# A bank of its own for the last products, and squares issued one block ahead, in a fused attention and expert kernel

## The chip, the cores and the metric

The kernel runs on one core of one Trainium2 chip. Its time is the device time of one execution in microseconds (us); lower is better. Before the change the median of three runs is 751.62 us (751.49 to 752.33).

## The reference

Three layers run one after the other in float32. First comes windowed and dilated attention over 4 batches, 8 heads and 576 positions, which gives `x` of 2304 tokens by 512. Then each token goes through one of eight experts. The last layer, which the change touches, is dense:

```
h = np.maximum(x @ w_in, 0.0)          # 2304 x 512 by 512 x 2048
return (h * h @ w_out).astype(np.float32)   # 2304 x 2048 by 2048 x 512
```

## The kernel before

Every matrix product is made exact enough by splitting each operand into a high part (rounded, by ScalarE) and a low part (the operand less its high part, by VectorE) and multiplying high by high, high by low and low by high: three matmuls for one (`mm3`, lines 814 to 816).

The dense layer has two stages. **The seven-product stage** computes `g = x @ w_in`, transposed, with a seven-product scheme on 2 by 2 blocks. It goes over six visits, each one half of the features for one of three blocks of 768 tokens. A visit has two double steps, and `strassen(d)` issues double step `d`, which handles two pairs of feature rows. A double step opens its own products ("now") and closes those of the one before it ("old"), so that engines have time between them; `strassen(12)` only closes: S3·T3 and A22·T4 of the last two pairs. A product is 6 matmuls of 384 columns. The eight PSUM banks are named in `bank(tag, n)`: four "b", two "c", two "d". S3·T3 accumulates into the pair's bank `pb`; `added` (line 1111) has VectorE add another tile to the bank, and stores the sum into the DRAM tensor `g_d`. Then A22·T4 accumulates into the same `pb`, and `kept` (line 1100) has ScalarE copy it out for a store. The "kept" tiles have three buffers, the tiles for the stores ("cr") eight.

**The second stage** multiplies `relu(g)` squared by `w_out`. `ORDER` lists 48 blocks, 16 feature blocks for each of the three token blocks, and the token block visited last comes last. `load_g` fetches a block of `g_d` (384 KB) into one of four buffers `gq`, on SyncE's queue (SP). `split_g` squares it in place on VectorE (line 1365), makes the high part on ScalarE (1366) and the low part on VectorE (1367), into one of three pairs of slots inside `slot_d`. `down2(n, j)` multiplies block n by the output weights of its feature block: for each of six columns of 128 tokens three matmuls of 512 columns (lines 1397 to 1399) into an `op` tile, of which there are eight, one in each bank. After 16 blocks the `op` tiles are copied out, half by VectorE and half by ScalarE, and scattered to the output by GpSimd (line 1407).

The output weights arrive as 64-bit numbers and are narrowed and split beside the products: `narrow1` on ScalarE (lines 1136 and 1137), `narrow2` and `narrow3` on VectorE (1143 to 1152), `out_hi` on ScalarE (1161), `out_lo` on VectorE (1166). In the seven-product stage `beside()` hands out these steps after each product. What is left goes to `finish_units(n)`, which issues the same number of steps in each of the second stage's first 14 blocks; the weights of feature block f are wanted by block f, the sixteenth by block 15.

The order of the work is written out by hand: each engine runs its instructions in the order in which this code issues them, and waits at an instruction until its inputs are there and its output's place is free. Thus `split_g(1)`, issued between `strassen(11)` and `strassen(12)`, stands in VectorE's and ScalarE's order ahead of all that `strassen(12)` asks of them; and within a block of the second stage the split of block n + 2 comes first, then the load of block n + 4, then the weight steps, then the matmuls of block n.

Of the kernel before, what the change touches and what calls it, by code (L numbers as in the profile page):

```python
# [10 lines left out]
F32 = mybir.dt.float32  # L11
# [5 lines left out]
ALU = mybir.AluOpType  # L17
# [49 lines left out]
def attention_experts_kernel(ctx: ExitStack, tc: tile.TileContext, qB, kB, vB, wg, wE, wF, consts, rows, ids, out):  # L67
    nc = tc.nc
# [691 lines left out]
    def experts():  # L760
# [329 lines left out]
        def bank(tag, n):  # L1090
            return ps2.tile([P, 512], F32, tag=tag, name=f"bank_{tag}", bufs=n)[:, :TB]

        def product(out, pair, a, n, b, first):
            wh, wl = left_t[pair, a]
            mh, ml = right(n, b)
            for i in range(2):
                o = slice(P * i, P * i + P)
                mm3(out, wh[:, o], wl[:, o], mh[:, i], ml[:, i], first and i == 0, i == 1, not first)

        def kept(bank, tag="kept"):  # L1100
            t = up_.tile([P, TB], F32, tag=tag, name=tag, bufs=8 if tag == "cr" else 3)
            nc.scalar.copy(out=t, in_=bank)
            return t

        def out_tile():
            return up_.tile([P, TB], F32, tag="cr", name="cr", bufs=8)

        def store_g(q, b, f, t):
            nc.sync.dma_start(out=g_d[b][P * f:P * f + P, TB * t:TB * t + TB], in_=q)

        def added(x, y, b, f, t):
            q = out_tile()
            nc.vector.tensor_tensor(out=q, in0=x, in1=y, op=ALU.add)  # L1113
            store_g(q, b, f, t)
# [12 lines left out]
        def load_next():  # L1127
            u = next(loaded64, None)
            if u is not None:
                load_64(*u, raw2)  # L1130
# [56 lines left out]
        def ready(n, name):  # L1187
            return n < 1 or name == "B12" or (n, name) in split
# [69 lines left out]
        def beside():  # L1258
            s = clock["slot"]
            for e in range(3):  # L1260
                credit[e] = min(credit[e] + RATE[e], 1.6)
            for lane in lanes:
                while lane.head is not None:
                    do, cost, gap, first = lane.head
                    if s < max(first, lane.last + gap) or any(c and credit[e] < min(c, 1.5) for e, c in enumerate(cost)):
                        break
                    lane.last = s
                    lane.pull()
                    do()
                    for e in range(3):  # L1270
                        credit[e] -= cost[e]
            clock["slot"] += 1

        def must(lane, done):
            while not done():
                do = lane.head[0]
                lane.last = clock["slot"]
                lane.pull()
                do()
# [3 lines left out]
        def strassen(d):  # L1283
            now = None
            if d < 2 * len(VISITS):
                b, half = VISITS[d // 2]
                now = dict(b=b, n=SETS[d // 2], pairs=[PAIRS * half + 2 * (d % 2) + i for i in range(2)], pb=[], pd=[], p5=[])
            old = prev.pop() if prev else None

            def use(x, i, out, a, b, first):  # L1290
                must(lanes[2], lambda: (x["pairs"][i], a) in left_t)
                must(lanes[1], lambda: ready(x["n"], b))
                product(out, x["pairs"][i], a, x["n"], b, first)

            if now:
                for i in range(2):
                    f = 2 * now["pairs"][i]
                    pb, pc = bank("b", 4), bank("c", 2)
                    now["pb"].append(pb)
                    use(now, i, pb, "A11", "B11", True)  # L1300
                    beside()
                    use(now, i, pc, "A12", "B21", True)
                    added(pc, kept(pb), now["b"], f, 0)
                    beside()
            if old:
                for i in range(2):
                    use(old, i, old["pb"][i], "S3", "T3", False)
                    added(old["pb"][i], old["p5"][i], old["b"], 2 * old["pairs"][i] + 1, 1)
                    beside()
            if now:  # L1310
                for i in range(2):
                    pd = bank("d", 2)
                    now["pd"].append(pd)
                    use(now, i, pd, "S1", "T1", True)
                    now["p5"].append(kept(pd, "p5"))
                    beside()
            if now:
                for i in range(2):
                    use(now, i, now["pb"][i], "S2", "T2", False)
                    beside()  # L1320
            if old:
                for i in range(2):
                    use(old, i, old["pb"][i], "A22", "T4", False)
                    store_g(kept(old["pb"][i], "cr"), old["b"], 2 * old["pairs"][i] + 1, 0)
                    beside()
            if now:
                for i in range(2):
                    use(now, i, now["pd"][i], "S4", "B22", False)
                    added(now["pd"][i], kept(now["pb"][i]), now["b"], 2 * now["pairs"][i], 1)
                    beside()  # L1330
                prev.append(now)
# [3 lines left out]
        def finish_units(n):  # L1335
            lane = lanes[2]
            todo = []
            while lane.head is not None:
                todo.append(lane.head[0])
                lane.pull()  # L1340
            rest.extend(todo)
            for _ in range(-(-len(rest) // max(14 - n, 1))):
                rest.pop(0)()
# [5 lines left out]
        ORDER = [(b, f) for b in reversed(range(NTP)) for f in range(16)]  # L1349
        gq_t, g_t = {}, {}  # L1350
        gp = None

        def load_g(n):
            if n < len(ORDER):
                b, f = ORDER[n]
                t = gp.tile([P, TP], F32, tag="gq", name="gq", bufs=4)
                nc.sync.dma_start(out=t, in_=g_d[b][P * f:P * f + P, :])
                gq_t[n] = t

        def split_g(n):  # L1360
            if n < len(ORDER):
                u = 6 + 2 * (n % 3)
                h, l = (flat_y[:, TP * (u + a):TP * (u + a) + TP] for a in range(2))
                x = gq_t.pop(n)
                nc.vector.scalar_tensor_tensor(out=x, in0=x, scalar=0.0, in1=x, op0=ALU.max, op1=ALU.mult)  # L1365
                nc.scalar.copy(out=h, in_=x)  # L1366
                nc.vector.tensor_tensor(out=l, in0=x, in1=h.bitcast(F32), op=ALU.subtract)  # L1367
                g_t[n] = (h, l)

        load_next()  # L1370
        load_next()
        for d in range(2 * len(VISITS)):
            strassen(d)
            if d == 10:
                load_g(3)
                split_g(0)
            if d == 9:
                yst.close()
                gp = ust.enter_context(tc.tile_pool(name="gp", bufs=1, side="right", reuse_waits="tile"))
                for n in range(3):  # L1380
                    load_g(n)
        split_g(1)
        strassen(2 * len(VISITS))
        pst.close()
        ps3 = st.enter_context(tc.tile_pool(name="ps3", bufs=1, space=PSUM, reuse_waits="tile"))

# [27 lines left out]

        JS = range(TP // P)
        for n in range(len(ORDER)):
            split_g(n + 2)
            load_g(n + 4)
            finish_units(n)
            if n + 2 < len(ORDER):  # L1420
                for j in JS:
                    down2(n, j)
# [76 lines left out]
    with tc.manual_schedule():  # L1499
        experts()  # L1500
# [85 lines left out]
```

## Time and profile before

| | |
|---|---|
| median of the runs | 751.62 us |
| the profiled execution, its own time | 755.42 us |
| its span, first to last instruction | 753.8 us |
| TensorE busy | 703.1 us, 93% |
| VectorE busy | 485.9 us, 64% |
| ScalarE busy | 328.0 us, 44% |
| mean granted TensorE clock | 0.97 |

The span is one execution as the hardware profiler recorded it. The share of an engine is the time in which it ran instructions of its kind; matmuls overlap their neighbours, so a busy TensorE is not one at its peak. The granted clock is the share of full speed that TensorE was allowed. The seven-product stage lies between about 356 and 539 us of the span, the second stage behind it, up to about 741 us.

### The profile page before, as it was taken

The numbers are of one execution on the slowest core, as the hardware profiler recorded it, in microseconds if no ns is written. First come the engines' busy times: TensorE is split into PE (matmuls) and PEld (weight loads), VectorE is DVE, ScalarE is ACT, GpSimd is POOL, SyncE is SP. The second block draws the span as 40 slices with busy tenths as digits, with TensorE's granted clock in tenths as the row PEclk, the third lists the DMA queues.
The fourth block names the chain that finished last, engine by engine and source line by source line (L and its number), as shares of the span: only waits on it lengthen the run. The fifth ranks groups of instructions, "written<-read, shape, count | busy, mean of one in ns | idle before, by whom it ended". The sixth has DMA issues, their size and how long they took to land. (4 is left out here: it accounts for less than half of the span.)

```text
span 753.8 us, 13877 instructions
## 1 busy us (share of the span) xinstructions
PE 703.1 (93%) x5227; PEld 639.2 (85%) x5227; DVE 485.9 (64%) x894; ACT 328.0 (44%) x601; POOL 113.5 (15%) x120
## 2 busy tenths in 40 slices
PE   7879379999999999999999999999899999999993
PEld 4657249999999999999999999999788778888882
DVE  7757446576566476678986877787577755445430
ACT  2534124464445555656555545555334322222110
POOL 5344422420110110008000000000000030011003
PEclk9989777999999999999999999999999999999997
DMA  8998564684756668663656654766544444334302
GB/s 274 324 255 248 162 217 121 215 243 146 232 177 207 206 191 248 214 219 83 219 166 231 194 170 156 255 194 214 179 151 157 135 165 127 105 118 154 99 8 87
DMA packets 67155, 136.90 MB, mean 182 GB/s; under 512 B 10857, under 2 KB 43498, under 8 KB 66058
## 3 DMA queue, kind: packets, MB, share of 16 engines
q1 hardware_dynamic: 57434, 120.09, 50.5%
q0 software_dynamic: 4176, 10.57, 4.1%
q10 hardware_dynamic: 5472, 5.29, 2.1%
q8 instruction: 43, 0.70, 0.4%
q14 instruction: 30, 0.25, 0.1%
HBM read 102.00 MB, written 33.96 MB: 180 GB/s over the span
## 5 line engine op out<-in xcount | busy, mean ns | idle before, releaser
L1367 DVE TENSOR_TENSOR slot_d<-gq,slot_d 128x768 fp32r<-128x768 f32 x48 | 46.0, 959 | 75.8 <-ACT slot_d L1366 75.8
L1366 ACT CAST slot_d<-gq 128x768 fp32r<-128x768 f32 x48 | 40.1, 835 | 111.4 <-PE op L1398 73.4
L1407 POOL DMA_INDIRECT out<-os,idc x18 | 19.6, 1088 | 363.9 <-DVE os L1406 359.5
L828 ACT ACTIVATE hh<-hp 128x240 fp32r<-128x240 f32 (+6 forms) x72 | 29.3, 408 | 42.4 <-PE hp L816 41.9
L158 POOL DMA_INDIRECT xg<-x_d,mt x23 | 25.3, 1101 | 142.5 <-PE xp L182 95.7
L1365 DVE SCALAR_TENSOR_TENSOR gq<-gq 128x768 f32<-128x768 f32 x48 | 45.6, 951 | 0.0
L1397 PE MATMUL op<-slot_b,slot_d 128*128 128x512 f32 x108 | 42.8, 396 | 1.4 <-ACT slot_b L1161 1.4
L1398 PE MATMUL op<-slot_b,slot_d 128*128 128x512 f32 x108 | 42.8, 396 | 0.9 <-DVE slot_b L1166 0.9
L1399 PE MATMUL op<-slot_b,slot_d 128*128 128x512 f32 x108 | 42.8, 396 | 0.0
L1397 PE MATMUL op<-slot_a,slot_d 128*128 128x512 f32 x108 | 42.0, 389 | 0.0
L1399 PE MATMUL op<-slot_a,slot_d 128*128 128x512 f32 x108 | 42.0, 389 | 0.0
L1398 PE MATMUL op<-slot_a,slot_d 128*128 128x512 f32 x108 | 42.0, 389 | 0.0
L140 DVE TENSOR_TENSOR slot_d<-raw,slot_d 128x1024 fp32r<-128x1024 f32 x24 | 29.3, 1226 | 19.7 <-ACT slot_d L139 19.7
L481 PE MATMUL o<-vb,pts 128*32 128x130 f32 x576 | 23.5, 298 | 19.2 <-DMA vb<-in_vB 14.6
L829 DVE SCALAR_TENSOR_TENSOR hl<-hp,hh 128x240 fp32r<-128x240 f32 (+6 forms) x72 | 31.2, 443 | 15.6 <-ACT hh L828 15.5
L481 PEld LDWEIGHTS o<-vb,pts 128*32 128x32 f32 x576 | 17.2, 117 | 23.1 <-issue 19.0
L843 ACT COPY ys<-yp 128x240 f32<-128x240 f32 (+6 forms) x36 | 14.3, 397 | 46.6 <-PE yp L816 46.5
L140 DVE TENSOR_TENSOR slot_b<-raw,slot_b 128x1024 fp32r<-128x1024 f32 x20 | 24.2, 1221 | 12.8 <-ACT slot_b L139 12.8
L814 PE MATMUL bank_b<-slot_d,slot_a 128*128 128x384 f32 x84 | 28.5, 340 | 3.8 <-DVE cr L1113 3.8
L814 PE MATMUL yp<-hh,slot_b 128*128 128x240 f32 (+3 forms) x112 | 31.9, 285 | 0.0
L815 PE MATMUL yp<-hl,slot_b 128*128 128x240 f32 (+3 forms) x112 | 31.7, 283 | 0.0
L816 PE MATMUL yp<-hh,slot_b 128*128 128x240 f32 (+3 forms) x112 | 31.6, 282 | 0.0
(323 smaller groups left out, 2316.7 us busy)
## 6 DMA issues: line engine op xcount, KB each, us to landing
raw<-in_wE SPq DMA_DIRECT2D x63, 512.0 KB
g_d<-cr SPq DMA_DIRECT2D x96, 192.0 KB
gq<-g_d SPq DMA_DIRECT2D x48, 384.0 KB
raw<-in_wF SPq DMA_DIRECT2D x32, 512.0 KB
vb<-in_vB SPq DMA_DIRECT2D x16, 520.0 KB
yr<-yT_d SPq DMA_DIRECT2D x16, 384.0 KB
q<-in_qB SPq DMA_DIRECT2D x8, 512.0 KB
x_d<-x SPq DMA_DIRECT2D x22, 128.0 KB
```

The costliest lines, as they stand in the source:

```text
L140: nc.vector.tensor_tensor(out=lo, in0=raw, in1=hi.bitcast(F32), op=ALU.subtract)
L481: nc.tensor.matmul(out=o[p // 2][32 * c:32 * c + 32, p % 2, 0:130], lhsT=pt[:, p, 32 * c:32 * c + 32], rhs=v[:, :, p, c, :], start=True, s ...
L814: nc.tensor.matmul(out=out, lhsT=wh, rhs=mh, start=first, stop=False, skip_group_check=shared)
L815: nc.tensor.matmul(out=out, lhsT=wh, rhs=ml, start=False, stop=False, skip_group_check=shared)
L816: nc.tensor.matmul(out=out, lhsT=wl, rhs=mh, start=False, stop=last, skip_group_check=shared)
L829: nc.vector.scalar_tensor_tensor(out=l[:, :n], in0=p[:, :n], scalar=0.0, in1=h[:, :n].bitcast(F32), op0=ALU.max, op1=ALU.subtract)
L1365: nc.vector.scalar_tensor_tensor(out=x, in0=x, scalar=0.0, in1=x, op0=ALU.max, op1=ALU.mult)
L1366: nc.scalar.copy(out=h, in_=x)
L1367: nc.vector.tensor_tensor(out=l, in0=x, in1=h.bitcast(F32), op=ALU.subtract)
L1397: nc.tensor.matmul(out=o_t[j], lhsT=h[:, a], rhs=w[:, 0], start=f == 0, stop=False)
L1398: nc.tensor.matmul(out=o_t[j], lhsT=h[:, a], rhs=w[:, 1], start=False, stop=False)
L1399: nc.tensor.matmul(out=o_t[j], lhsT=l[:, a], rhs=w[:, 0], start=False, stop=f == 15)
```

## The change

It has two parts. In `strassen(12)`, where nothing new is opened, A22·T4 gets a "c" bank and starts a sum there in place of going on in `pb`. ScalarE copies the bank of S3·T3 into a "kept" tile (`u3`) once S3·T3 is done, and VectorE adds that tile to the new bank and stores the sum.

In the second stage the square leaves `split_g` and becomes `square_g`; `split_g` issues the high part and hands back the low part as a function, so that its caller can put something between them. The main loop now issues the high part of block n + 2, the square of block n + 3, the low part of block n + 2 and the load of block n + 5. Ahead of the loop block 1 is squared at the end of `strassen(10)`, and its split, the square of block 2 and the load of block 4 come after `strassen(12)`; before, the split of block 1 came ahead of it.

```
             if old:
                 for i in range(2):
                     use(old, i, old["pb"][i], "S3", "T3", False)
                     added(old["pb"][i], old["p5"][i], old["b"], 2 * old["pairs"][i] + 1, 1)
+                    if not now:
+                        u3.append(kept(old["pb"][i]))
                     beside()
...
-                    use(old, i, old["pb"][i], "A22", "T4", False)
-                    store_g(kept(old["pb"][i], "cr"), old["b"], 2 * old["pairs"][i] + 1, 0)
+                    if now:
+                        use(old, i, old["pb"][i], "A22", "T4", False)
+                        store_g(kept(old["pb"][i], "cr"), old["b"], 2 * old["pairs"][i] + 1, 0)
+                    else:
+                        pc = bank("c", 2)
+                        use(old, i, pc, "A22", "T4", True)
+                        added(pc, u3[i], old["b"], 2 * old["pairs"][i] + 1, 0)
...
+        def square_g(n):
+            if n < len(ORDER):
+                x = gq_t[n]
+                nc.vector.scalar_tensor_tensor(out=x, in0=x, scalar=0.0, in1=x, op0=ALU.max, op1=ALU.mult)
+
         def split_g(n):
             if n < len(ORDER):
...
-                nc.vector.scalar_tensor_tensor(out=x, in0=x, scalar=0.0, in1=x, op0=ALU.max, op1=ALU.mult)
                 nc.scalar.copy(out=h, in_=x)
-                nc.vector.tensor_tensor(out=l, in0=x, in1=h.bitcast(F32), op=ALU.subtract)
                 g_t[n] = (h, l)
+                return lambda: nc.vector.tensor_tensor(out=l, in0=x, in1=h.bitcast(F32), op=ALU.subtract)
+            return lambda: None
...
             if d == 10:
                 load_g(3)
-                split_g(0)
+                square_g(0)
+                split_g(0)()
+                square_g(1)
...
-        split_g(1)
         strassen(2 * len(VISITS))
+        lo = split_g(1)
+        square_g(2)
+        lo()
+        load_g(4)
...
         for n in range(len(ORDER)):
-            split_g(n + 2)
-            load_g(n + 4)
+            lo = split_g(n + 2)
+            square_g(n + 3)
+            lo()
+            load_g(n + 5)
             finish_units(n)
```

## Rows read from the trace of the kernel before

**Rows 1.** The page, parts 1 (busy us, share) and 2 (slices; granted clock in tenths).
```profile
PE 703.1 (93%) x5227; PEld 639.2 (85%) x5227; DVE 485.9 (64%) x894; ACT 328.0 (44%) x601; POOL 113.5 (15%) x120
...
PEclk9989777999999999999999999999999999999997
```

**Rows 2.** Waits of TensorE, whole span: total us, times, longest.
```profile
PE bank_b L814 <- DVE cr L1113: 3.8, 1, 3.8
...
PE op L1397 <- ACT slot_b L1161: 1.4, 1, 1.4
```

**Rows 3.** Timeline of TensorE at the last products: start, us, instruction, [idle before <-releaser].
```profile
532.00 0.34 PE L816 MATMUL bank_b<-slot_d,slot_b 128*128 128x384 f32 x1
536.10 0.44 PE L814 MATMUL bank_b<-slot_d,slot_a 128*128 128x384 f32 x1 [3.77 <-DVE cr L1113]
...
539.22 0.63 PE L1397 MATMUL op<-wo,slot_d 128*128 128x512 f32 x1
...
540.50 0.44 PE L1397 MATMUL op<-wo,slot_d 128*128 128x512 f32 x1
```

**Rows 4.** Timeline of VectorE in the same stretch.
```profile
532.16 0.69 DVE L1152 CUSTOM_DVE_ANT_0 fp<-fa,fl 128x1024 uint16<-128x1024 uint16 x1
532.77 0.95 DVE L1365 SCALAR_TENSOR_TENSOR gq<-gq 128x768 f32<-128x768 f32 x1
534.62 0.96 DVE L1367 TENSOR_TENSOR slot_d<-gq,slot_d 128x768 fp32r<-128x768 f32 x1 [0.90 <-ACT slot_d L1366]
535.50 1.02 DVE L1113 TENSOR_TENSOR cr<-bank_b,p 128x384 f32<-128x384 f32 x2
```

**Rows 5.** Windows: us; PE, PEld, DVE, ACT, POOL busy; clock; DMA share; GB/s.
```profile
537.30:540.50 3.20, 3.20 (x10) 2.92 (x10) 0.08 (x1) 1.52 (x3) 0.00 (x0) 0.50 0.39 140
545.00:590.00 45.00, 45.00 (x201) 37.22 (x200) 34.08 (x50) 17.87 (x27) 0.00 (x0) 1.00 0.45 155
553.50:555.50 2.00, 2.00 (x10) 1.67 (x9) 1.45 (x2) 0.52 (x1) 0.00 (x0) 1.00 0.00 0
605.60:608.40 2.80, 2.80 (x8) 2.23 (x7) 1.83 (x2) 0.83 (x2) 0.00 (x0) 0.50 0.06 9
615.00:735.00 120.00, 120.00 (x532) 99.34 (x531) 57.87 (x65) 27.42 (x34) 10.55 (x9) 1.00 0.35 108
```

**Rows 6.** Timeline of TensorE in the second stage.
```profile
598.14 0.50 PE L1398 MATMUL op<-slot_b,slot_d 128*128 128x512 f32 x1 [0.71 <-DVE slot_b L1166]
...
603.72 0.50 PE L1397 MATMUL op<-slot_b,slot_d 128*128 128x512 f32 x1 [1.43 <-ACT slot_b L1161]
604.45 0.50 PE L1398 MATMUL op<-slot_b,slot_d 128*128 128x512 f32 x1 [0.23 <-DVE slot_b L1166]
...
609.84 0.39 PE L1399 MATMUL op<-slot_b,slot_d 128*128 128x512 f32 x1
...
740.42 0.39 PE L1399 MATMUL op<-slot_b,slot_d 128*128 128x512 f32 x1
```

**Rows 7.** Groups of VectorE, 545 to 590: busy us, mean ns, idle before, releaser.
```profile
L1367 DVE TENSOR_TENSOR slot_d<-gq,slot_d 128x768 fp32r<-128x768 f32 x10 | 9.6, 959 | 10.5 <-ACT slot_d L1366 10.5
L1365 DVE SCALAR_TENSOR_TENSOR gq<-gq 128x768 f32<-128x768 f32 x10 | 9.5, 951 | 0.0
...
L1166 DVE TENSOR_TENSOR slot_a<-fp,slot_a 128x512 fp32r<-128x512 f32 x5 | 3.4, 687 | 1.4 <-ACT slot_a L1161 1.4
```

**Rows 8.** Groups of ScalarE, 545 to 590.
```profile
L1366 ACT CAST slot_d<-gq 128x768 fp32r<-128x768 f32 x9 | 7.5, 834 | 15.8 <-DVE gq L1365 13.6 <-PE op L1398 2.2
```

**Rows 9.** Timeline of VectorE in `strassen(11)`.
```profile
522.35 0.55 DVE L1113 TENSOR_TENSOR cr<-bank_c,kept 128x384 f32<-128x384 f32 x1
522.81 0.55 DVE L1113 TENSOR_TENSOR cr<-bank_b,p 128x384 f32<-128x384 f32 x1
```

**Rows 10.** Timeline of TensorE in `strassen(11)`: the first A22·T4.
```profile
525.93 0.33 PE L814 MATMUL bank_b<-slot_d,slot_c 128*128 128x384 f32 x1
```

**Rows 11.** Timeline of the SP queue in the second stage.
```profile
547.34 0.33 SPq L808 DMA_DIRECT2D raw<-in_wF  x1
```

More of the change, by code (lines that the diff above doesn't have):

```diff
@@ L1288, in strassen @@
             old = prev.pop() if prev else None
+            u3 = []
             def use(x, i, out, a, b, first):
```

## The prediction

> **What bounds the kernel now.** I read the page first, then the waits, then timelines at the waits. TensorE is busy 93% of the span and runs near its full clock in every slice but the first eight and the last [rows 1]; so time can be won only where TensorE stands still, or runs at the lower clock because it stood still. The waits of TensorE over the whole program [rows 2] show which stops the change can touch: one of 3.8 us at the end of the seven-product stage (bank_b, behind an add of line 1113), and one of 1.4 us in the second stage (op, behind the split of the output weights, line 1161), with two small ones beside it that line 1166 ended; the others lie in earlier stages and stay.
>
> The first stop: the last matmul of the two S3·T3 products starts at 532.00, the first of A22·T4 at 536.10 after 3.77 us of idleness [rows 3]. A22·T4 accumulates into the bank of S3·T3, so the adds that read that bank have to be done. VectorE meanwhile squares block 1 (532.77), waits 0.90 us for ScalarE's high part, subtracts (534.62), and only at 535.50 comes to the two adds [rows 4]: split_g(1) is issued ahead of strassen(12). After the stop the clock falls: the stretch from 537.3 to 540.5 ran at 0.50, the 1.2 GHz level [rows 5].
>
> The second group of stops is a pace that is too slow. From 545 to 590 TensorE never idles [rows 5]; from the end of the second group of stops on, 32 blocks of 18 matmuls start between 609.84 and 740.42 [rows 6], 226.7 ns each; at that a step of 18 is 4.08 us, and TensorE did 11.0 of them in the 45 us. VectorE did 10 squares and 10 subtractions there, 4.5 us a block, and was idle 10.5 us of them waiting for ScalarE's high part [rows 7], while ScalarE waited 13.6 us for the square [rows 8]: square, high part, low part run as one chain, and behind it on VectorE stand the steps that make the output weights. So VectorE loses some 0.4 us a step, and the weights of steps 14 and 15 are late: stops of 0.71 us (598.14), 1.43 us (603.72) and 0.23 us (604.45) [rows 6]. Then the clock is at 0.50 again from 605.6 to 608.4 [rows 5].
>
> **The change part by part.**
>
> *The drain.* From 525.93 to 532.00 lie 35 starts of 384 columns [rows 3, 10], 0.173 us each. Without any wait A22·T4 would start so much behind 532.00, at 532.17; its 12 matmuls of 0.173 us take 2.08 us, and the second stage would start at 534.25 instead of 539.22 [rows 3]: 4.97 us. This holds 3.77 us of idleness; the rest, 1.2 us, is the restart and the lower clock. Three op matmuls then took 0.43 us each (539.22 to 540.50, 1.28 us [rows 3]) where 0.68 are due: 0.60 us more, and 0.05 for the next. Sum 5.62 us.
>
> Does a new wait take its place? A22·T4 now opens a group in a "c" bank. The last reader of the two c banks is the add that starts at 522.35 and takes 0.55 us [rows 9], 9 us before 532.17: nothing. In the second stage the banks are reused at once: op tiles 2 and 3 lie on S3·T3's banks and tiles 4 and 5 on the c banks. VectorE is free at 532.85 (end of the last row of weight work, 532.16 + 0.69 [rows 4]); two adds of 0.47 us from start to start bring it to 533.8, the adds of A22·T4 end near 534.3 and 535.1, since its products end near 533.5 and 534.45. Tile 4 is wanted at 534.25 + 4 × 0.68 = 536.97, tile 5 at 537.65: 2.5 us of cover. The copy of S3·T3 on ScalarE now reads the same bank as the add. If they are ordered one behind the other, it moves to some 533.4 and 533.8 and its add by as much, still ahead of 536.97; between nothing and 0.6 us on ScalarE, nothing on TensorE.
>
> *First splits later.* Block 1 was split ahead of the drain; now its high part (0.83 us [rows 8]) follows the two copies, to be done by 534 to 535, and its low part follows the square of block 2: 535.1 + 0.87 + 0.96 = 536.9. Step 1 wants it at 534.25 + 4.08 = 538.3, its first use in the third matmul. Cover 1.4 us; without it TensorE would wait for the rest. Load 4 goes behind the last stores on the SP queue, as before, and some 5 us earlier.
>
> *The square of block 1* moves into the end of strassen(10). It takes 0.95 us of VectorE ahead of the adds at 522.35 and 522.81, which release the banks that the older A22·T4 wants at 525.93 [rows 9, 10]. The second add ends at 523.4, with the square at 524.3 at the latest: 1.6 us left, so nothing; without that cover up to 0.95 us.
>
> *The second stage's order.* Squares no longer stand between a step's start and its high part, and the 10.5 us of waits of [rows 7] are filled with the next block's square. VectorE's work per block is then (45 − 10.5)/10 = 3.45 us, of which 0.14 are waits for a weight's high part (1.4 us in ten blocks [rows 7]); twice that would make it 3.6, still below TensorE's 4.08. ScalarE's high part can't start before TensorE leaves the slot, at the start of the step, so the low part ends about 1.8 us into the step, and two or three weight steps (2 to 2.6 us) behind it end about 4.4 us into the step. VectorE starts a step at most about 1.5 us late and catches up in those with less work. The weights for step 14 are finished in step 12 and those for step 15 in step 13 (42 pending steps, three in each of 14 steps), about 3.5 us ahead of TensorE. All three stops go. Their whole cost: from the first start of op to the last are 863 intervals (48 blocks of 18 less one); at 226.7 ns they are 195.64 us, against 201.20 measured, 539.22 to 740.42 [rows 3, 6]: 5.56 us over, of which 0.65 are counted in the drain; 4.91 us are left. Idleness 2.37, the lower clock about 1.5 (2.8 us at 0.50 give back 1.4 [rows 5]), the restarts the rest.
>
> What is late next: nothing on TensorE; from the drain on it would run without a stop. Tail, copies and stores shift as a block.
>
> *SP's queue.* Load n+5 replaces n+4 but waits for a buffer freed one step earlier in the order, so issue to use stays some two steps, 8 us. The nearest rows: issues from 547.34 on (a 512 KB load and two of 384 KB) have moved all bytes by 553.5, when the DMA engines show nothing more [rows 5, 11]: 6.2 us for three, so between nothing and, if a load landed later, a wait of VectorE that still has a step of cover.
>
> *Sum.* 5.62 + 4.91 = 10.5 us. The profiled execution took 755.42 us (span 753.8 and 1.6 around it), so 744.9 there. It is 3.8 us above the median of 751.62, and no view says where; the stops are waits of one engine for another, so I take the gain off the median unchanged: 741.1 us.
>
> **Rivals.**
>
> 1. *The second fall of the clock stays.* It follows three short stops, far shorter than the one of the drain, so its cause may be another. Then 1.4 to 1.6 us come back: 742.6. For it: 0.50 after so little idleness. Against: 545 to 590 and 615 to 735 run without idleness at 1.00 [rows 5]. The Trainium skill (TensorE: Matmul & The Clock Gate, "Why this matters for your kernels") blames one long idle gap between bursts of matmuls for a lost clock; the drain's fall agrees with that (3.77 us, then 0.50), the second does not, and by that rule alone this rival would be the forecast. The sum stands on the rows without idleness.
>
> 2. *The weights stay late.* If VectorE keeps 4.5 us a block, because the low part, tied to TensorE's step through the slot, makes the weight steps behind it late, the stop at step 15 is set by VectorE, which starts only some 1.5 us earlier (its square of block 2 at 535.0 instead of 536.4 behind the adds [rows 4]): the drain's gain becomes a longer wait, 1.5 to 2.5 us in all, 749.5. With half of the pace won, 745.
>
> 3. *The drain is not freed*: some reader of the new bank or of the c banks holds A22·T4. Then only the 4.91 remain: 746.7. Against it: 9 us of cover.
>
> 4. *Slower: a square that waits for its load.* The square of n+3 now stands ahead of the low part of n+2 in VectorE's order, so a load that lands late holds a block that is two steps nearer its use. It decides when loads land more than some 14 us after issue, or when 384 KB and three fifths of 512 KB a step (691 KB) don't fit in 4.08 us. At the 140 GB/s that the stretch behind the drain shows [rows 5] a step would be 5.05 us, 0.97 over, for 14 steps 13.6 us: 754.7 against the forecast's 741.1. Against: the same loads fit now, with DMA at 0.45 [rows 5].
>
> **How the numbers follow.** Forecast 0.66, rival 1 0.08, half of the pace (745) 0.09, rival 3 0.06, rival 2 whole 0.05, nothing at all 0.02, rival 4 0.04. Faster by over 0.2% (what a measurement here can tell from no change, 1.5 us) are the first five: 0.94; within 0.2% 0.02; slower 0.04. The range goes from 740.0 (0.6 us of restarts and copies more than summed, and the 0.5 us that runs differ) to 747.0, which takes in rivals 1, 3 and half of 2, and leaves out 0.11 above.
>
> **What would show it.** Right: no wait of TensorE for line 1113 or lines 1161 and 1166; A22·T4 in bank_c starting 0.17 us behind S3·T3; no stretch at 0.50 from 530 to 735; op's first and last matmul 195.6 us apart; VectorE's waits for the high part gone or moved to ScalarE waiting for op. Wrong: a new wait of op for slot_d (low part of block 1, rival 4), stops at steps 14 and 15 (rival 2), or a fall of the clock without a stop (rival 1).

## The result and the profile after

| | before | after |
|---|---|---|
| median | 751.56 us (750.69 to 752.33, 6 runs) | 742.05 us (739.70 to 744.74, 6 runs) |
| ratio after to before, 95% interval | | 0.9877 (0.9861 to 0.9893) |
| the profiled execution, its own time | 755.42 us | 742.29 us |
| its span | 753.8 us | 740.5 us |
| first product of the seven-product stage to last matmul of the second, in the trace | 383.47 us | 372.91 us |
| the same, less short stops that are no part of the change (below) | 382.85 us | 372.91 us |

The change is faster by 9.5 us of the median; 10.5 were forecast, 741.1 against 742.05. The last two rows of the table are free of what happens ahead of the changed stages. The stretch before runs from 356.95, the first matmul into a "b" bank, to 740.42 [rows 6], after from 354.22 to 727.13. The first product, and the first of S3·T3, which is wanted later, before:

```profile
356.95 0.34 PE L814 MATMUL bank_b<-slot_d,slot_a 128*128 128x384 f32 x1
...
530.09 0.33 PE L814 MATMUL bank_b<-slot_d,slot_b 128*128 128x384 f32 x1
```

The first profile of before holds some short stops between 402 and 411 us, too short for the list of waits. In TensorE's timeline of before, starts that should be 0.17 us apart are 0.31 and 0.36 us apart:

```profile
402.04 0.34 PE L816 MATMUL bank_c<-slot_d,slot_b 128*128 128x384 f32 x1
402.35 0.44 PE L814 MATMUL bank_b<-slot_d,slot_a 128*128 128x384 f32 x1
...
409.64 0.34 PE L816 MATMUL bank_b<-slot_d,slot_a 128*128 128x384 f32 x1
410.00 0.44 PE L814 MATMUL bank_b<-slot_d,slot_a 128*128 128x384 f32 x1
```

With the slow intervals behind them they are 0.62 us in sum. Nothing that the change touches is near, and other profiles hold between nothing and 0.56 us of them, so they are taken off below. Such a sum takes in the intervals that stand out, and is good to some 0.1 us. Net of them the stretch is 9.94 us shorter.

The timeline of TensorE after, which answers to [rows 3] and to the end of [rows 6]:

```profile
354.22 0.34 PE L814 MATMUL bank_b<-slot_d,slot_a 128*128 128x384 f32 x1
...
526.51 0.34 PE L816 MATMUL bank_d<-slot_d,slot_b 128*128 128x384 f32 x1
527.20 0.44 PE L814 MATMUL bank_b<-slot_d,slot_b 128*128 128x384 f32 x1 [0.35 <-ACT kept L1102]
...
529.40 0.33 PE L814 MATMUL bank_c<-slot_d,slot_a 128*128 128x384 f32 x1
...
531.48 0.39 PE L1415 MATMUL op<-wo,slot_d 128*128 128x512 f32 x1
...
727.13 0.39 PE L1417 MATMUL op<-slot_b,slot_d 128*128 128x512 f32 x1
```

A22·T4 (529.40, now in bank_c) starts 0.17 us behind the last of S3·T3, with no stop, and the second stage begins 2.08 us later. From its first to its last start are 195.65 us; 195.64 were due at 226.7 ns. One small stop is new: S3·T3 waits 0.35 us behind a kept copy.

The waits of TensorE from 500 us to the end of the second stage, which answer to [rows 2], are that one alone:

```profile
PE bank_b L814 <- ACT kept L1102: 0.3, 1, 0.3
```

VectorE's timeline after, for [rows 4]: the four adds of the drain come first, then square of block 2, low part of block 1, and so on in turn.

```profile
529.63 0.69 DVE L1152 CUSTOM_DVE_ANT_0 fp<-fa,fl 128x1024 uint16<-128x1024 uint16 x1
530.24 1.01 DVE L1113 TENSOR_TENSOR cr<-bank_b,p 128x384 f32<-128x384 f32 x2
531.39 1.02 DVE L1113 TENSOR_TENSOR cr<-bank_c,kept 128x384 f32<-128x384 f32 x2
532.33 0.95 DVE L1371 SCALAR_TENSOR_TENSOR gq<-gq 128x768 f32<-128x768 f32 x1
533.20 0.95 DVE L1380 TENSOR_TENSOR slot_d<-gq,slot_d 128x768 fp32r<-128x768 f32 x1
534.06 0.95 DVE L1371 SCALAR_TENSOR_TENSOR gq<-gq 128x768 f32<-128x768 f32 x1
...
537.57 0.96 DVE L1371 SCALAR_TENSOR_TENSOR gq<-gq 128x768 f32<-128x768 f32 x1 [1.08 <-DMA gq<-g_d]
```

Windows of the second stage after (columns as in [rows 5]; the clock is the third column from the right) and VectorE's groups from 537 to 582, for [rows 7]:

```profile
532.00:590.00 58.00, 58.00 (x258) 48.01 (x256) 50.61 (x74) 26.95 (x41) 0.00 (x0) 1.00 0.55 181
590.00:607.00 17.00, 17.00 (x77) 14.08 (x75) 10.03 (x13) 5.01 (x7) 6.98 (x6) 1.00 0.49 164
607.00:727.00 120.00, 120.00 (x531) 99.41 (x530) 52.21 (x59) 25.41 (x32) 10.48 (x10) 1.00 0.33 102
```

```profile
L1380 DVE TENSOR_TENSOR slot_d<-gq,slot_d 128x768 fp32r<-128x768 f32 x12 | 11.5, 955 | 3.0 <-ACT slot_d L1378 2.9
L1371 DVE SCALAR_TENSOR_TENSOR gq<-gq 128x768 f32<-128x768 f32 x12 | 11.4, 952 | 1.1 <-DMA gq<-g_d 1.1
```

TensorE neither idles nor loses its clock. In 45 us VectorE now has 12 blocks in hand where it had 10, and waits 2.9 us for the high part where it waited 10.5.

### The profile page after: what moved, and what is told of

Read it like the earlier page. It is cut to its first block, busy times and chain, and to the rows that moved or that the text cites. A ratio compares the mean times of both kernels' runs of the same rounds, so it can differ in the third digit from the quotient of the medians.

```text
span 740.5 us, 13891 instructions
## 1 busy us (share of the span) xinstructions
PE 695.3 (94%) x5227; PEld 634.6 (86%) x5227; DVE 486.7 (66%) x896; ACT 327.2 (44%) x601; POOL 114.4 (15%) x120
## 5 line engine op out<-in xcount | busy, mean ns | idle before, releaser
L1415 PE MATMUL op<-slot_b,slot_d 128*128 128x512 f32 x108 | 42.0, 389 | 0.0
L1416 PE MATMUL op<-slot_b,slot_d 128*128 128x512 f32 x108 | 42.0, 389 | 0.0
L1417 PE MATMUL op<-slot_b,slot_d 128*128 128x512 f32 x108 | 42.0, 389 | 0.0
L140 DVE TENSOR_TENSOR slot_b<-raw,slot_b 128x1024 fp32r<-128x1024 f32 x20 | 24.3, 1223 | 14.6 <-ACT slot_b L139 14.5
L1102 ACT COPY kept<-bank_b 128x384 f32<-128x384 f32 x50 | 23.4, 486 | 14.9 <-PE bank_b L816 11.5
```

Of the source, the lines that this page charges most:

```text
L140: nc.vector.tensor_tensor(out=lo, in0=raw, in1=hi.bitcast(F32), op=ALU.subtract)
L1415: nc.tensor.matmul(out=o_t[j], lhsT=h[:, a], rhs=w[:, 0], start=f == 0, stop=False)
L1416: nc.tensor.matmul(out=o_t[j], lhsT=h[:, a], rhs=w[:, 1], start=False, stop=False)
L1417: nc.tensor.matmul(out=o_t[j], lhsT=l[:, a], rhs=w[:, 0], start=False, stop=f == 15)
```

## The experiments

The "net stretch" runs from the first product of the seven-product stage to the last matmul of the second stage in one profile, less the short stops between 399 and 411 us, whose sum is given where there are any. It was 382.85 before and 372.91 after. "The drain" is what `strassen(12)` does. A ratio compares a run with executions of the kernel before that were taken beside it; their median was 751.86 us for runs 1 to 4, 753.49 for 5 to 8 and 753.02 for 9 to 11.

**1. The drain's part alone.** The square stays in `split_g`, the loop is the one of before.

```
...
+                        pc = bank("c", 2)
+                        use(old, i, pc, "A22", "T4", True)
+                        added(pc, u3[i], ...)
...
-        split_g(1)
         strassen(2 * len(VISITS))
+        split_g(1)
```

> Own bank for the last A22T4 and block 1 split behind strassen(12), whole; the second stage's loop as before (square, high part, low part as one chain). Theory (the parts need each other): the drain's stop of 3.77 us goes and the second stage starts some 5 us earlier, but VectorE still needs about 4.5 us a block, starts only about 2 us earlier, and the weights of steps 14 and 15 come late by more: stops there of 5 to 6 us in place of 2.4, and a gain of 2 to 2.5 us only, 749.3. Rival (the parts add): the stops at steps 14 and 15 keep their 2.4 us, gain 5.6, 746.

Measured: ratio 0.9983 (0.9955 to 1.0011), net stretch 381.00 (0.28 taken off), a gain of 1.85 us, which the times alone can't tell from none. The first op comes 177.02 us after the first product (182.27 before, 177.26 after the change), but the second stage grows from 201.20 to 204.26. Waits of TensorE from 500 us on:

```profile
PE op L1405 <- ACT slot_b L1161: 1.4, 1, 1.4
PE op L1405 <- ACT slot_d L1374: 1.3, 3, 0.6
PE op L1406 <- DVE slot_b L1166: 1.1, 2, 0.8
PE op L1407 <- DVE slot_d L1375: 1.0, 4, 0.3
```

```profile
L1375 DVE TENSOR_TENSOR slot_d<-gq,slot_d 128x768 fp32r<-128x768 f32 x10 | 9.6, 959 | 9.7 <-ACT slot_d L1374 9.7
```

The second fence is VectorE from 540 to 585: 10 blocks in 45 us, as before. So the theory holds in cause and nearly in size (2 to 2.5 expected), but not in place: the stops at steps 14 and 15 are no longer than before (1.4 and 1.1 us). The rest has become seven short stops for slot_d, since VectorE is now so late that the split of a block itself comes too late: five of them lie ahead of step 14 (563.99 to 587.32) and two at step 18 (615.76 and 616.76).

**2. The new loop alone.** The drain is left as it was.

```
-        split_g(1)
+        square_g(1)
+        split_g(1)()
         strassen(2 * len(VISITS))
+        square_g(2)
+        load_g(4)
...
         for n in range(len(ORDER)):
-            split_g(n + 2)
-            load_g(n + 4)
+            lo = split_g(n + 2)
+            square_g(n + 3)
+            lo()
+            load_g(n + 5)
```

> The new order of the second stage's loop with squares one block ahead; A22T4 in the old bank and block 1 squared and split ahead of strassen(12), as before. Theory: the drain keeps its stop of about 3.8 us and the low clock behind it, VectorE's waits for the high part go, no stop at steps 14 and 15 and no second fall of the clock: gain 4.9, 746.7. Rival (the second fall of the clock has another cause): clock at 0.50 again near 600 us, gain 3.3, 748.2. Rival (VectorE stays late): stops at step 15 remain, gain under 2.

Measured: ratio 0.9949 (0.9930 to 0.9969), net stretch 377.86, a gain of 4.99 us; forecast 4.9. The only wait of TensorE left is the drain's, and the second stage takes 195.65 us at full clock:

```profile
PE bank_b L814 <- DVE cr L1113: 3.8, 1, 3.8
```

```profile
531.60:533.00 1.40, 1.38 (x4) 1.38 (x5) 1.40 (x3) 0.00 (x0) 0.00 (x0) 0.50 0.41 147
...
538.00:600.00 62.00, 62.00 (x276) 51.34 (x275) 50.49 (x73) 26.50 (x40) 0.69 (x1) 1.00 0.47 159
600.00:725.00 125.00, 125.00 (x553) 103.56 (x552) 56.72 (x64) 27.20 (x35) 13.27 (x12) 1.00 0.35 110
```

The second fall of the clock went with the stops, so nothing that stays brings it about by itself. The low clock behind the drain began here as soon as TensorE restarted (0.50 from 531.6). Gains of 1.85 and 4.99 make 6.84 us; both parts together bring 9.94. The drain's gain counts in full only where VectorE keeps up.

**3. The own bank alone.** Nothing else is changed: A22·T4 goes into a "c" bank, the split of block 1 stays ahead of `strassen(12)`.

```
...
+                        pc = bank("c", 2)
+                        use(old, i, pc, "A22", "T4", True)
+                        added(pc, u3[i], ...)
...
         split_g(1)
         strassen(2 * len(VISITS))
```

> Own bank for the last A22T4 alone; split of block 1 ahead of strassen(12) and the loop as before. Theory: A22T4 follows S3T3 without a stop though VectorE's adds come late as before (535.5); then op tiles 2 to 5 wait about 0.5 to 1 us in all for the late adds to release their banks; then the weights are late as in the run with the whole drain: gain about 2, 749.5, with stops of 5 us at steps 14 and 15. Rival (the parts add): 746.5.

Measured: ratio 0.9972 (0.9952 to 0.9992), net stretch 380.77, a gain of 2.08 us. The stop of the drain is gone; one of 1.22 us for an op tile (533.92, behind the adds) has come, 0.2 more than expected, and the weights and splits are late as in the first run (1.4, 1.1, 0.8 and 0.7 us). So the gain is the expected one, but the stops at steps 14 and 15 sum to 2.5 us and not to 5; the rest is short stops for slot_d again. The parts don't add.

**4. The changed kernel again.**

> The changed kernel unchanged, for a second profile and more times. Theory: from the first matmul of the seven-product stage to the last of the second stage the trace shows about 372.9 us again (383.4 before), and the scatter of the times of some 5 us lies ahead of that stage. Rival: the scatter lies in the changed stages, and that stretch differs by over 1 us between the two profiles.

Measured: 740.62 us, ratio 0.9846 (0.9816 to 0.9877). The two ends of the stretch:

```profile
352.50 0.34 PE L814 MATMUL bank_b<-slot_d,slot_a 128*128 128x384 f32 x1
...
725.42 0.39 PE L1417 MATMUL op<-slot_b,slot_d 128*128 128x512 f32 x1
```

372.92 us, with nothing to take off, within 0.01 of the first profile. In all the profiles of this study, with the same instructions ahead of that stage, its first product starts between 351.95 and 357.33 us. What of a profiled execution's own time lies neither ahead of that start nor in the stretch is 14.6 to 15.2 us in every one. So the scatter of the profiled executions lies ahead of the stage; of the others only the time is known.

**5. The square of block 1 later.** The changed kernel, with one line moved.

```
                 split_g(0)()
-                square_g(1)
...
         strassen(2 * len(VISITS))
+        square_g(1)
         lo = split_g(1)
```

> The changed kernel with the square of block 1 moved from the end of strassen(10) to behind strassen(12), just ahead of its split. Theory: the new stop of 0.35 us of S3T3 behind a kept copy comes from that square, which made VectorE's weight steps and with them ScalarE's queue 0.87 us late; it goes, and the stretch from the first matmul of the seven-product stage to the last of the second shrinks from 372.9 to 372.3. The high part of block 1 is then ready some 0.9 us and its low part 0.4 us before TensorE wants them. Rival: ScalarE is late there for another reason, the stop stays, 372.9; or the low part comes late, a stop of op behind slot_d of 0.2 to 0.5 us and 372.9.

Measured: 741.28 us, ratio 0.9854 (0.9815 to 0.9893); net stretch 372.29, no wait of TensorE from 500 us on. ScalarE's queue here, to be held against the one under "What failed" below:

```profile
522.42 0.62 ACT L1161 CAST slot_b<-fp 128x512 fp32r<-128x512 f32 x1 [1.85 <-DVE fp L1152]
...
524.78 0.87 ACT L1102 COPY kept<-bank_b 128x384 f32<-128x384 f32 x2
```

Counted from the first product (353.23 here, 354.22 there), `out_hi` begins 0.86 us and the kept copies 0.89 us sooner. As the theory had it to 0.01 us: the new stop came from that square. The times can't tell it from the changed kernel; the net stretch can, by 0.62 us.

**6. Without the own bank.** The changed kernel with A22·T4 back in S3·T3's bank; late split and new loop stay.

```
-                        pc = bank("c", 2)
-                        use(old, i, pc, "A22", "T4", True)
+                        use(old, i, old["pb"][i], "A22", "T4", False)
...
```

> The changed kernel without the own bank: A22T4 accumulates in the bank of S3T3 as before, with the late split and the new loop kept. Theory: most of the drain's stop was the split of block 1 standing ahead of the adds; with the split behind, the first add ends 1.3 us after A22T4 could start, so a stop of about 1.3 us stays there and the stretch is 374.4 instead of 372.9; no fall of the clock. Rival: the bank carries the drain, stop 3.8 us, 377.9.

Measured: 743.88 us, ratio 0.9892 (0.9851 to 0.9933), net stretch 374.48.

```profile
530.38 0.44 PE L814 MATMUL bank_b<-slot_d,slot_a 128*128 128x384 f32 x1 [1.29 <-DVE cr L1113]
```

The stop is 1.29 us, and the clock stays at 1.00 behind it. With the late split in place the own bank is worth 1.6 us.

**7. The split ahead, with the own bank.**

```
+        split_g(1)()
         strassen(2 * len(VISITS))
-        lo = split_g(1)
         square_g(2)
-        lo()
```

> The changed kernel with the split of block 1 back ahead of strassen(12), own bank and new loop kept. Theory: with a bank of its own A22T4 does not ask for the adds, so the order of the split costs TensorE nothing: the op tile on the first old bank is wanted about 0.6 us after its late release; stretch 372.9. Rival: the late split is needed too, because op tiles 2 to 5 wait for adds that come 0.9 us later: a stop of op behind the adds or the kept copies of 0.3 to 1.2 us, as in the run with the own bank alone, and 373.3 to 374.3.

Measured: 742.48 us, ratio 0.9870 (0.9828 to 0.9913), net stretch 372.94 (0.56 taken off). No op tile waits, and from the start of S3·T3 to the first op are 4.27 us, against 4.28 in the changed kernel. So the theory holds: with the own bank, and block 1 squared early, the place of its split is free. Either cure of the drain does most of it alone, and the two overlap.

**8. Loads one step nearer.**

```
         lo()
-        load_g(4)
...
-            load_g(n + 5)
+            load_g(n + 4)
```

> The changed kernel with load n+4 in place of n+5 in block n of the second stage, so one step less between the issue of a load and its square. Theory (a late load has a step of cover): VectorE waits for loads at the square, up to 1.5 us at a time and under 8 us in all over the second stage, TensorE has no new stop, stretch 372.9. Rival (a square that waits for its load holds the low part ahead of TensorE): stops of op behind slot_d, stretch over 374.

Measured: 741.49 us in its one execution, net stretch 372.94 (0.26 taken off). VectorE's wait for loads from 525 us on, first here and then after the change:

```profile
DVE gq L1371 <- DMA gq<-g_d: 3.9, 5, 1.5
```

```profile
DVE gq L1371 <- DMA gq<-g_d: 1.1, 1, 1.1
```

A late load does hold VectorE at the square, up to 1.5 us, and a step of cover swallows it: no new stop of TensorE. The slower rival is real in its first half, the wait at the square, and far from deciding.

**9. The low part ahead of the next square.**

```
-            lo = split_g(n + 2)
+            split_g(n + 2)()
             square_g(n + 3)
-            lo()
```

> The changed kernel with the square of block n+3 issued behind the low part of block n+2, not between its high and low part. Theory: what counts is that the square is done a step early, so that the high part can start when the slot is free and is ready when VectorE, late from its weight steps, comes to the low part; filling the wait is not needed. No stop of TensorE in the second stage, stretch 372.9, VectorE's waits for the high part in the weight steps' 13 blocks a few us longer than in the changed kernel (7 us there). Rival: the filled wait is what counts; VectorE loses 0.9 us a block again, stops at steps 14 and 15 of 2 us or more, stretch over 375.

Measured: 740.84 us, ratio 0.9861 (0.9820 to 0.9902), net stretch 372.92 (0.12 taken off); no stop in the second stage. VectorE from 535 to 580, first here and then in the changed kernel's second profile:

```profile
L1380 DVE TENSOR_TENSOR slot_d<-gq,slot_d 128x768 fp32r<-128x768 f32 x11 | 10.5, 957 | 4.1 <-ACT slot_d L1378 4.0
```

```profile
L1380 DVE TENSOR_TENSOR slot_d<-gq,slot_d 128x768 fp32r<-128x768 f32 x11 | 10.5, 954 | 2.8 <-ACT slot_d L1378 2.7
```

That the square is a step early is what counts; that it fills a wait brings 1.3 us of VectorE's time in 45, and no time of the kernel.

**10. The square of block 1 ahead of the drain's adds.** As in 5, but the line stands ahead of `strassen(12)`.

> The changed kernel with the square of block 1 ahead of strassen(12) in place of behind strassen(10). Theory: the stop behind the kept copy goes, as with the square behind strassen(12), but the adds of the drain come 0.9 us later, ScalarE's copies behind them end at about the moment at which the third op tile wants the bank: between no stop and 0.2 us of op; stretch 372.3 to 372.5. Rival: the late adds hold TensorE for over 0.3 us, 372.9 or more.

Measured: 739.55 us in its one execution, net stretch 372.29, no stop. Both places do the same.

**11. The kernel before again.**

> The kernel before, for a second profile. Theory (the same three stops bring the same fall of the clock): stops of 0.7, 1.4 and 0.2 us at steps 14 and 15, granted clock 0.50 for about 3 us behind them, stretch 383.4. Rival (where the fall comes is chance, as the run with the whole drain and the one with the own bank had the same stops and kept 1.00): the stops without the fall, stretch about 382.

Measured: 750.25 us in its one execution, net stretch 382.88 (0.11 taken off), within 0.03 of the first profile, with the same three stops (0.80, 1.41 and 0.23 us) and the same fall behind them:

```profile
597.00:600.00 3.00, 1.35 (x5) 0.63 (x4) 2.28 (x4) 0.62 (x1) 0.00 (x0) 1.00 0.48 131
600.00:603.00 3.00, 3.00 (x9) 2.32 (x8) 2.02 (x3) 0.83 (x1) 0.00 (x0) 0.52 0.00 0
```

In this kernel the fall comes with the stops, in two profiles of two. Why the runs with the drain's part alone and with the own bank alone kept 1.00 behind the same three stops is open. One difference is on record: both of them lack the drain's long stop, and with it the first fall. The second fall is seen only where both kinds of stops stand, and no run tells whether it needs both.

## Why the prediction was right

- **The drain's stop and its price.** Forecast 4.97 us up to the first op. From the first start of S3·T3 (530.09 before, 527.20 after) to the first op it was 9.13 and is 4.28, and 0.11 of the 4.28 is the restart of the new stop: 4.96. Runs 3 and 6 show that the cause was read rightly: A22·T4 no longer asks for the adds, and they no longer stand behind the split. But of two cures that I summed as one, either takes most of it once the new loop is in place (runs 6 and 7).
- **The second stage.** Forecast 5.56 us over what 863 intervals need; it went from 201.20 to 195.65. VectorE's pace was the cause (runs 1, 2 and 9). The rivals of weights that stay late and of a clock that falls anyway are out (run 2).
- **The copies and adds on one bank** are ordered, as the step allowed for: ScalarE stands idle for 3.35 us until VectorE's first add is done. The first product was there at 528.51 (528.18 + 0.33), so the order behind the add makes up about 2.4 us of it. It costs TensorE nothing:

```profile
528.18 0.33 PE L816 MATMUL bank_b<-slot_d,slot_b 128*128 128x384 f32 x1
...
526.66 0.86 ACT L1102 COPY kept<-bank_b 128x384 f32<-128x384 f32 x2
530.88 0.95 ACT L1102 COPY kept<-bank_b 128x384 f32<-128x384 f32 x2 [3.35 <-DVE cr L1113]
```

- **What failed: "the square of block 1 ... so nothing".** I took VectorE's adds and their 1.6 us of cover as all that stands behind that square. Behind it also stand `narrow3`, and behind this on ScalarE `out_hi`, two steps of `narrow1` and the copies that S3·T3 wants (526.66 above, 0.02 us ahead of the moment at which TensorE wanted the bank). The links of that chain, VectorE first:

```profile
523.55 0.69 DVE L1152 CUSTOM_DVE_ANT_0 fp<-fa,fl 128x1024 uint16<-128x1024 uint16 x1
524.27 0.62 ACT L1161 CAST slot_b<-fp 128x512 fp32r<-128x512 f32 x1 [1.84 <-DVE fp L1152]
...
525.17 0.67 ACT L1136 ACTIVATE fa<-raw 128x512 f32<-128x512 f32 x1
525.75 0.65 ACT L1137 ACTIVATE fl<-raw 128x512 int32<-128x512 uint32 x1
526.30 0.46 ACT L1102 COPY cr<-bank_b 128x384 f32<-128x384 f32 x1
```

  So a term put at nothing measured 0.62 us (0.51 to the late start, 0.11 of restart; run 5 gives back 0.62).
- **The sum.** 10.53 us forecast less the 0.62 that I left out are 9.91; the net stretch lost 9.94. The medians lost 9.5 here and 11.2 in run 4 (751.86 to 740.62), which differ from it by no more than the scatter ahead of the changed stages. I allowed 0.5 us for what runs differ, from three of them; the twelve executions of the changed kernel lie between 736.70 and 744.74. That the median came within 1 us of the forecast therefore owes something to luck, and it is the stretch in the trace that bears the sum out.

## What to carry to other kernels

A stop of the bound engine is worth its length only if the stages behind can take the earlier start: read the pace of the helper engine in the next stage (blocks done in a window against steps done by the bound engine) before counting it. Where square, high part and low part run as one chain across two engines, issuing the first link a step early frees the pace without removing any work. And when an instruction is put into an engine's order, follow not only its own engine's queue but the other engine's queue that waits for it.

## What the runs showed of the hardware

A stop costs more than the idle time that the trace names: the 0.35 us at 527.20 cost 0.62, since the next start is also late by what matmuls otherwise overlap (0.16) and by a slower first interval (0.28 for 0.17). The lower clock came behind the 3.77 us stop in three profiles of three, but at different moments: at once in run 2 (0.50 from 531.6), 0.7 to 0.8 us after the restart at 531.08 in run 11, and 1.0 to 1.1 us after the one at 536.10 in the first profile of before. The windows of run 11 and of that profile (the clock is the third column from the right):

```profile
531.10:531.80 0.70, 0.70 (x4) 0.70 (x5) 0.70 (x2) 0.00 (x0) 0.00 (x0) 1.00 0.00 0
531.90:535.20 3.30, 3.30 (x11) 3.20 (x11) 0.46 (x1) 0.96 (x3) 0.00 (x0) 0.50 0.49 176
```

```profile
536.10:537.10 1.00, 1.00 (x6) 1.00 (x7) 1.00 (x2) 0.00 (x0) 0.00 (x0) 1.00 0.20 71
537.20:540.50 3.30, 3.30 (x11) 3.02 (x10) 0.18 (x1) 1.52 (x3) 0.00 (x0) 0.50 0.41 147
```

Behind the 1.29 us stop of run 6 it stayed at 1.00. Behind the three stops at steps 14 and 15 it fell in both profiles of before and in neither of runs 1 and 3. The Trainium skill (TensorE: Matmul & The Clock Gate, "Why this matters for your kernels") blames one long idle gap between bursts of matmuls; the drain's stop agrees with that each time, the three short stops of before do not.
